# Value products leave PSUM only behind the next pair's global scores, in an order that is searched anew

## The chip, the cores and the metric

One core of one Trainium2 chip runs the kernel. The metric is the device time of one execution in microseconds (us). TensorE (PE) multiplies matrices, VectorE (DVE) and ScalarE (ACT) work elementwise and read PE's results from the eight banks of PSUM, GpSimd (POOL) works elementwise on SBUF only, and SyncE (SP) issues nearly all DMAs from one queue, in order.

## The reference

Eight batches of 8 heads have 512 local and 32 global tokens, head dimension 64. Global tokens attend to all tokens, a local token to the global ones and to its window of 32 to either side. The 4,352 rows of 512 numbers that come out pass an FFN.

```python
s_g = scale * np.matmul(q_g, k_all.transpose(0, 1, 3, 2))
out_g = np.matmul(sm(s_g), v_all)
s_ll = scale * np.matmul(q_l, k_l.transpose(0, 1, 3, 2))
mask = np.abs(pos[:, None] - pos[None, :]) <= window
s_ll = np.where(mask, s_ll, -1000000000.0)
s_lg = scale * np.matmul(q_l, k_g.transpose(0, 1, 3, 2))
a_l = sm(np.concatenate([s_lg, s_ll], axis=-1))
out_l = np.matmul(a_l, np.concatenate([v_g, v_l], axis=2))
...
x = np.ascontiguousarray(attn_out.transpose(0, 2, 1, 3)).reshape(B * S, H * D)
h = x @ w_in
g = h - np.tanh(h)
return (g @ w_out).astype(np.float32)
```

## The kernel before

**Two kinds of work on PE.** The FFN of a batch ("chunk") has steps of 12 matmuls each of 128x512: a step of the hidden layer, H (L1188), and a step of the output layer, O (L1236). Each product is made in three passes from a high and a low half (`x_hi`, `x_lo`, `w_in_hi`, `w_in_lo` and so on). The chunk of batch b runs between the attention steps of batch b+1. Attention goes by pairs of heads. Batches 0 and 1 use the class `Pair`: scores L641, transposes L661, global scores L578, products L738. Batches 2 to 7 use `WindowPair`, and there PE does a **visit** once per pair as one unbroken piece: the value products of the pair in two halves (L1044), then the scores (L874) and the global scores (L896) of the next pair. Between two visits stand 76 to 104 H and O matmuls.

**The banks.** PSUM has two pools: four banks for attention and for H steps, four for the accumulators of O. A visit takes all four of the first: two for the products' halves (named o), two for the scores (s). The global scores of the next pair are written to other columns of the two o banks. A bank goes to an H step when all its readers are done.

**Behind a visit.** `add_output` takes a half of the products out: `high` casts it to `x_hi` (a copy, L368, on ACT or DVE), `rest` subtracts to make `x_lo` (L1077, DVE) and keeps the columns of global tokens in `xg` (L1079, L1081). DVE then finds the peaks of scores (L974) and of global scores (L908), ACT takes exponentials (L982, L938), POOL multiplies by the inverse sums (L996), DVE turns the probabilities (L1014, L963) for the next products. For each H step ACT computes tanh (L1196), DVE subtracts (L1199), ACT or DVE casts `ghi` (L368) and POOL subtracts `glo` (L1205).

**The start.** Weights come in packed pieces: load (L430), rebias on ACT (L437), two shifts on DVE (L441, L445), a cast for the high half (L368) and a subtraction on POOL for the low half (L451). The pieces go through few buffers (`first_q`, `stage`, `wpair`, `wraw`). All of batch 0's attention comes before the first H step.

**What sets the order.** A greedy list scheduler (class `Order`) takes all operations with modelled durations, dependencies (`r`, `w`), banks and buffers, and at each step puts the one that can start first, ties and preferences being set by due times. The due times and penalties come from the table `CFG` of about 190 numbers. In 5 to 72 us of its own clock, where it finds PE without work, it puts dummy matmuls (`fill`, L1843); a fixed number of them stands with the first H step.

**Leaving.** Each chunk's four accumulators are copied out (to halves of `wpair`, two free at a time) and stored by SP (L1264), behind whatever stands in its queue ahead of them: loads of values (L1095 to L1098) and of keys and queries (L843).

## Time and profile before

| | |
|---|---|
| median of 3 runs | 926.34 us (924.04 to 926.7) |
| profiled execution, its own time | 926.6 us |
| span of its profile | 924.8 us |
| PE busy | 908.7 us |
| DVE busy | 703.3 us |
| ACT busy | 409.8 us |
| POOL busy | 331.7 us |
| mean granted clock of TensorE | 0.998 |

The span runs from the first to the last instruction; 1.8 us of the execution lie outside. In the rows below a line of a timeline has start, duration, engine, line, operation, output<-input, and in brackets the idle time before it with what ended it.

### The profile page before, as it was taken

How to read it: one execution, taken by the hardware profiler on the slowest of the kernel's cores; microseconds unless marked ns; L12 is line 12 of the kernel's file. 1: busy time of each engine (PE TensorE's matmuls, PEld its weight loads, DVE VectorE, ACT ScalarE, POOL GpSimd, SP SyncE). 2: the span in 40 equal slices, each digit the busy share in tenths (PEclk: the TensorE clock that was granted, in tenths of full speed). 3: DMA queues.
4: the chain of work that ended last, by engine and by line, in shares of the span. 5: the costliest groups of instructions: out<-in, count | busy, mean ns of one | idle time of the engine just before them, and what ended most of it. 6: DMA issues, size and time to landing. Idle time of an engine off the chain costs nothing.

```text
span 924.8 us, 21774 instructions
## 1 busy us (share of the span) xinstructions
PE 908.7 (98%) x7839; PEld 749.1 (81%) x7839; DVE 703.3 (76%) x2268; ACT 409.8 (44%) x1178; POOL 331.7 (36%) x531
## 2 busy tenths in 40 slices
PE   7989999999999999999999999999999999999998
PEld 5667877788887788878888888888888888898986
DVE  5987776478887877877778787777778787888773
ACT  5976656444344333443334233433334343433232
POOL 3577765733333333332333333333323333110000
PEclk9999999999999999999999999999999999999999
DMA  9556343433234323342324233432324211100001
GB/s 227 143 158 190 117 123 88 95 87 63 59 76 110 64 51 68 63 116 48 62 52 106 51 66 68 98 76 47 71 52 105 48 43 27 46 1 1 1 0 69
DMA packets 248173, 70.13 MB, mean 76 GB/s; under 512 B 232704, under 2 KB 241408, under 8 KB 248064
## 3 DMA queue, kind: packets, MB, share of 16 engines
q1 hardware_dynamic: 246720, 68.21, 31.9%
q8 instruction: 62, 1.02, 0.5%
q10 hardware_dynamic: 1344, 0.52, 0.2%
q14 instruction: 47, 0.39, 0.1%
HBM read 59.77 MB, written 8.91 MB: 74 GB/s over the span
## 4 chain that ended last, share of the span: by engine, by line
PE 91%; DVE 4%; ACT 2%; DMA 1%; SPq 1%; issue 1%; POOL 0%; ACTq 0%; DVEq 0%; POOLq 0%
PE bank L1236 32%; PE bank L1188 31%; PE bank L1561 7%; PE bank L1681 6%; PE bank L1044 5%; PE bank L874 3%; DVE keys_first L1014 2%; PE bank L896 1%; PE bank L641 1%; PE bank L738 1%; PE bank L1587 1%; PE bank L661 1%; PE bank L545 1%; DMA first_raw<-in_q_l_dram 0%; DMA wpair<-in_moe_w_out_dram 0%
## 5 line engine op out<-in xcount | busy, mean ns | idle before, releaser
L1205 POOL TENSOR_TENSOR glo<-t,ghi 128x512 fp32r<-128x512 f32 x112 | 145.6, 1300 | 331.6 <-PE bank L1236 230.1
L1014 DVE STREAM_TRANSPOSE keys_first<-prob 32x256 f32<-32x256 f32 x384 | 167.3, 436 | 9.4 <-POOL prob L996 3.1
L1196 ACT ACTIVATE t<-bank 128x512 f32<-128x512 f32 x112 | 66.9, 597 | 176.9 <-PE bank L1188 162.6
L1236 PE MATMUL bank<-w_out_hi,ghi 128*128 128x512 f32 x448 | 125.0, 392 | 0.7 <-ACT wpair L368 0.7
L1236 PE MATMUL bank<-w_out_hi,glo 128*128 128x512 f32 x448 | 125.0, 393 | 0.1
L1236 PE MATMUL bank<-w_out_lo,ghi 128*128 128x512 f32 x448 | 124.7, 393 | 0.0
L1188 PE MATMUL bank<-x_hi,w_in_hi 128*128 128x512 f32 x448 | 120.6, 391 | 0.9 <-DVE st L974 0.5
L1188 PE MATMUL bank<-x_hi,w_in_lo 128*128 128x512 f32 x448 | 120.2, 390 | 0.0
L1188 PE MATMUL bank<-x_lo,w_in_hi 128*128 128x512 f32 x448 | 120.0, 390 | 0.0
L1199 DVE TENSOR_TENSOR t<-bank,t 128x512 f32<-128x512 f32 x112 | 77.0, 689 | 54.6 <-ACT t L1196 53.1
L368 ACT CAST ghi<-t 128x512 fp32r<-128x512 f32 (+1 forms) x100 | 61.4, 614 | 108.5 <-PE bank L1236 84.1
L1236 PEld LDWEIGHTS bank<-w_out_hi,ghi 128*128 128x128 f32 x448 | 83.3, 188 | 19.9 <-ACT wpair L368 1.4
L1188 PEld LDWEIGHTS bank<-x_hi,w_in_hi 128*128 128x128 f32 x448 | 83.7, 188 | 19.3 <-ACT wpair L437 0.8
L1188 PEld LDWEIGHTS bank<-x_lo,w_in_hi 128*128 128x128 f32 x448 | 84.0, 188 | 18.0 <-issue 0.5
L1236 PEld LDWEIGHTS bank<-w_out_hi,glo 128*128 128x128 f32 x448 | 83.1, 188 | 18.7 <-issue 1.0
L1188 PEld LDWEIGHTS bank<-x_hi,w_in_lo 128*128 128x128 f32 x448 | 83.9, 188 | 17.7 <-issue 0.2
L1236 PEld LDWEIGHTS bank<-w_out_lo,ghi 128*128 128x128 f32 x448 | 83.2, 188 | 18.2 <-issue 0.5
L996 POOL TENSOR_SCALAR prob<-prob,st 128x128 f32<-128x128 f32 x192 | 68.2, 372 | 75.8 <-DVE st L989 48.1
L982 ACT ACTIVATE prob<-prob,st 128x128 f32<-128x128 f32 x192 | 74.7, 391 | 3.6 <-DVE st L974 3.5
L1077 DVE TENSOR_TENSOR x_lo<-bank,x_hi 128x256 fp32r<-128x256 f32 x48 | 20.4, 424 | 49.4 <-ACT x_hi L368 49.4
L1044 PEld LDWEIGHTS bank<-keys_first,values 128*64 128x64 f32 x672 | 42.3, 138 | 9.8 <-DVE t L1199 5.3
L974 DVE CUSTOM_DVE_ANT_0 prob<-bank,wraw 128x128 f32<-128x128 f32 x192 | 45.7, 284 | 4.2 <-PE bank L874 1.6
(250 smaller groups left out, 1512.1 us busy)
## 6 DMA issues: line engine op xcount, KB each, us to landing
out_dram<-wpair SPq DMA_DIRECT2D x28, 256.0 KB, 2.2
rawkq<-in_q_l_dram SPq DMA_DIRECT2D x96, 64.0 KB, 2.3
rawkq<-in_k_l_dram SPq DMA_DIRECT2D x96, 64.0 KB, 2.3
stage<-in_moe_w_out_dram SPq DMA_DIRECT2D x6, 512.0 KB, 4.1
wpair<-in_moe_w_out_dram SPq DMA_DIRECT2D x6, 512.0 KB, 4.1
first_q<-in_moe_w_in_dram SPq DMA_DIRECT2D x6, 512.0 KB, 4.0
stage<-in_moe_w_in_dram SPq DMA_DIRECT2D x6, 512.0 KB, 3.8
values<-in_v_l_dram SPq DMA_DIRECT2D x24, 120.0 KB, 2.3
```

The costliest lines, as they stand in the source:

```text
L368: (nc.scalar.copy if e == "A" else nc.vector.tensor_copy)(dst, src)
L982: nc.scalar.activation(x, x, AF.Exp, bias=s[:, k:k + 1], scale=-1.0, accum_out=s[:, 8 + k:9 + k])
L996: nc.gpsimd.tensor_scalar(x, x, s[:, k:k + 1], 1.0, op0=ALU.mult, op1=ALU.mult)
L1014: nc.vector.transpose(view(win_kf[W * k:W * k + W], [(CH, 2), (P, NT), (1, W)], 3 * G + W * i), src)
L1044: nc.tensor.matmul(dst, win_values[h][:, window(b)], src, start=n == 0, stop=n == len(parts) - 1, skip_group_check=True)
L1188: nc.tensor.matmul(self.h[s][:, j * n:(j + 1) * n], w[:, cc, f * P:(f + 1) * P], self.x()[xi][:, cc, :n], start=part == 0 and cc == 0 and ...
L1196: nc.scalar.activation(tt_[q], self.h[s], AF.Tanh)
L1199: nc.vector.tensor_sub(tt_[q], self.h.pop(s), tt_[q])
L1205: eng[e].tensor_sub(gg[q][1], tt_[q], f32(gg[q][0]))
L1236: nc.tensor.matmul(self.acc[tt], g[:, j * self.n + tt * P:j * self.n + (tt + 1) * P], low_out(f) if wi else high_out(f), start=s == 0 and ...
L1561: nc.tensor.matmul(self.hold(tt, tags), g(), low_out(f) if wi else high_out(f), start=first and k < len(tts), stop=last and k == len(mms) - 1)
L1681: nc.tensor.matmul(dst[:, at], w, m, start=fresh and n == 1, stop=n == 6, skip_group_check=True)
```

## The change

`add_output` gives `high` and `rest` one more operand to wait for: the global scores of the next pair in the same half, where the next pair is of the same batch (`self.jj < 3`). And all numbers of `CFG` are replaced; the core of the diff is below, with one line of the table. One line is added in the code ahead of some places, so that from there on line numbers of the kernel after are one higher (L1189 for L1188, L1237 for L1236).

```diff
-               d_w=0.3761, d_wl=0.2437, d_wn=2.1507, d_xg=1.1595, d_y=3, gfirst=0.0, ho=7017.2009, hs=875.1568, lag=-190.1483,
+               d_w=0.3712, d_wl=0.2437, d_wn=1.8044, d_xg=1.1595, d_y=2.7078, gfirst=0.0, ho=34202.7904, hs=620.2931, lag=-1618.121,
...
             due = self.after(18.0)
-            add(either(256, "ph", True), high, due + 8 * 0.5, r=[o], w=[k + (0,) for k in x])
-            add(("D", 0.6), rest, due + 8 * 1, r=[o] + [k + (0,) for k in x],
+            behind = [("sg", self.j + 1, half)] if self.jj < 3 else []
+            add(either(256, "ph", True), high, due + 8 * 0.5, r=[o] + behind, w=[k + (0,) for k in x])
+            add(("D", 0.6), rest, due + 8 * 1, r=[o] + behind + [k + (0,) for k in x],
```

What the change does to the order is seen in three places.

On DVE, behind a visit of batch 5 whose next pair is of the same batch, before:

```order
L1199 TENSOR_TENSOR t_68<-bank_99,t_68 128x512
L1077 TENSOR_TENSOR x_lo_108<-bank_100,x_hi_107 128x256
L1081 COPY xg<-bank_100 128x32
L1077 TENSOR_TENSOR x_lo_108<-bank_98,x_hi_107 128x256
L1079 TENSOR_TENSOR xg<-bank_98,xg 128x32
L974 ISA prob,st_93<-bank_101,wraw_2008 128x128
L974 ISA st_93 128x1
...
L908 ISA pg,st_93<-bank_100,wraw_2008 128x192
L908 ISA st_93 128x1
L368 CAST ghi_70<-t_68 128x512
```

and after:

```order
L1200 TENSOR_TENSOR t_68<-bank_98,t_68 128x512
L974 ISA prob,st_93<-bank_99,wraw_1989 128x128
L974 ISA st_93 128x1
...
L1077 TENSOR_TENSOR x_lo_108<-bank_101,x_hi_107 128x256
L1081 COPY xg<-bank_101 128x32
L368 CAST ghi_70<-t_68 128x512
L1077 TENSOR_TENSOR x_lo_108<-bank_100,x_hi_107 128x256
L1079 TENSOR_TENSOR xg<-bank_100,xg 128x32
L908 ISA pg,st_93<-bank_101,wraw_1989 128x192
L908 ISA st_93 128x1
```

The subtractions L1077 stood ahead of the four peaks L974 and now stand behind them, ahead of the peaks L908 of the global scores.

On PE, at the first H step (`x_hi_87` is batch 0's activations; L661 and L641 are transposes and scores of a pair of batch 1), before:

```order
L616 MATMUL bank_98<-idr,pg 128x64 x6
...
L1843 MATMUL bank_101<-mask_90 128x224
...
L1188 MATMUL bank_101<-x_hi_87,w_in_hi 128x512 x4
L1188 MATMUL bank_101<-x_lo_88,w_in_hi 128x512 x4
L661 MATMUL bank_100<-idr,prob 128x64
...
L1188 MATMUL bank_101<-x_hi_87,w_in_lo 128x512 x4
L641 MATMUL bank_98<-first_kw_63,first_q_84 128x224
...
L1188 MATMUL bank_99<-x_hi_87,w_in_hi 128x512 x4
```

and after:

```order
L616 MATMUL bank_100<-idr,pg 128x64 x6
L661 MATMUL bank_99<-idr,prob 128x64
...
L641 MATMUL bank_101<-first_kw_63,first_q_84 128x224
...
L1844 MATMUL bank_99<-mask_90 128x224
...
L1189 MATMUL bank_99<-x_hi_87,w_in_hi 128x512 x4
L1189 MATMUL bank_99<-x_lo_88,w_in_hi 128x512 x4
L1189 MATMUL bank_99<-x_hi_87,w_in_lo 128x512 x4
L1189 MATMUL bank_98<-x_hi_87,w_in_hi 128x512 x4
L1189 MATMUL bank_98<-x_lo_88,w_in_hi 128x512 x4
L1189 MATMUL bank_98<-x_hi_87,w_in_lo 128x512 x4
```

A set of transposes and a pair of scores stand ahead of the first H step and no longer inside it; two H steps follow on each other. Over the whole start there are 65 dummy matmuls ahead of the first H step, in ten places, and 81 in eight before.

On PE, between the last O step of batch 0's chunk (`w_out_hi_1492`, after `w_out_hi_1600`, is the last piece of the weights) and the first O step of batch 1's (its four accumulators are the banks 102 to 105), before:

```order
L1236 MATMUL bank_103<-w_out_hi_1492,glo_71 128x512
L1188 MATMUL bank_100<-x_hi_107,w_in_hi 128x512 x4
L1188 MATMUL bank_100<-x_lo_108,w_in_hi 128x512 x4
L1188 MATMUL bank_100<-x_hi_107,w_in_lo 128x512 x4
L1188 MATMUL bank_99<-x_hi_107,w_in_hi 128x512 x4
...
L1188 MATMUL bank_99<-x_hi_107,w_in_lo 128x512 x4
L1236 MATMUL bank_105<-w_out_hi,ghi_72 128x512
L1236 MATMUL bank_104<-w_out_hi,ghi_72 128x512
L1236 MATMUL bank_102<-w_out_hi,ghi_72 128x512
L1236 MATMUL bank_103<-w_out_hi,ghi_72 128x512
```

and after:

```order
L1237 MATMUL bank_105<-w_out_hi_1600,ghi_70 128x512
...
L1237 MATMUL bank_104<-w_out_hi_1600,glo_71 128x512
L874 MATMUL bank_98<-first_m,hi_106 32x128
...
L896 MATMUL bank_100<-first_m,win_gq 32x2x64
...
L1237 MATMUL bank_103<-w_out_hi,ghi_72 128x512
L1237 MATMUL bank_102<-w_out_hi,ghi_72 128x512
L1237 MATMUL bank_105<-w_out_hi,ghi_72 128x512
L1237 MATMUL bank_104<-w_out_hi,ghi_72 128x512
```

Two H steps lay between the two O steps, now a set of scores (L874) and global scores (L896) does. On SP's queue the rows around the stores of batch 0's chunk are the same in both.

## Rows read from the trace of the kernel before

**Rows 1.** The page, part 1: busy time, share, instructions.
```profile
PE 908.7 (98%) x7839; PEld 749.1 (81%) x7839; DVE 703.3 (76%) x2268; ACT 409.8 (44%) x1178; POOL 331.7 (36%) x531
```

**Rows 2.** Stretches: length, busy PE, PEld, DVE, ACT, POOL, PEclk, DMA share, GB/s.
```profile
0.00:50.00 50.00, 40.79 (x404) 29.76 (x405) 37.36 (x165) 38.43 (x127) 26.38 (x59) 1.00 0.72 172
50.00:100.00 50.00, 49.49 (x322) 38.76 (x322) 40.30 (x89) 33.56 (x78) 34.57 (x33) 0.97 0.61 174
```

**Rows 3.** Timeline of TensorE ahead of and at the first FFN step.
```profile
58.38 1.90 PE L1843 MATMUL bank<-mask 128*128 128x224 bf16 x18
60.05 0.94 PE L1188 MATMUL bank<-x_hi,w_in_hi 128*128 128x512 f32 x3
```

**Rows 4.** Waits of TensorE: us in total, times, longest.
```profile
PE bank L545 <- DMA first_raw<-in_k_l_dram: 4.3, 1, 4.3
...
PE bank L1236 <- ACT wpair L368: 0.7, 2, 0.3
PE bank L1044 <- DVE keys_first L1014: 0.6, 1, 0.6
...
PE bank L1188 <- ACT wpair L437: 0.4, 1, 0.4
```

**Rows 5.** Chain in a visit of batch 5, TensorE: start, us, what.
```profile
531.42 1.09 PE bank L874 x64
532.50 0.55 PE bank L896 x25
...
535.09 1.13 PE bank L1188 x5
```

**Rows 6.** Timeline of ScalarE in this visit: start, us, instruction.
```profile
530.60 0.37 ACT L368 CAST x_hi<-bank 128x256 fp32r<-128x256 f32 x1 [2.18 <-PE bank L1044]
```

**Rows 7.** Timeline of VectorE in this visit.
```profile
531.00 0.42 DVE L1077 TENSOR_TENSOR x_lo<-bank,x_hi 128x256 fp32r<-128x256 f32 x1 [1.86 <-ACT x_hi L368]
...
531.90 0.42 DVE L1077 TENSOR_TENSOR x_lo<-bank,x_hi 128x256 fp32r<-128x256 f32 x1 [0.34 <-ACT x_hi L368]
...
532.54 0.29 DVE L974 CUSTOM_DVE_ANT_0 prob<-bank,wraw 128x128 f32<-128x128 f32 x1
...
533.39 0.35 DVE L908 CUSTOM_DVE_ANT_0 pg<-bank,wraw 128x192 f32<-128x192 f32 x1
...
534.90 0.08 DVE L908 DVE_READ_ACCUMULATOR2_ANT st<- 128x1 f32 x1
```

**Rows 8.** Stretches between two visits, columns as in rows 2.
```profile
257.15:278.11 20.96, 20.96 (x229) 17.35 (x228) 18.60 (x69) 9.29 (x30) 7.50 (x13) 1.00 0.46 92
...
427.47:452.06 24.59, 24.59 (x245) 20.35 (x245) 19.80 (x72) 9.42 (x30) 8.08 (x14) 1.00 0.29 57
```

**Rows 9.** Timeline of TensorE: last products, first output step of batch 1.
```profile
172.40 1.10 PE L738 MATMUL bank<-keys_first,values 128*64 128x160 f32 x16
...
188.09 1.07 PE L1188 MATMUL bank<-x_hi,w_in_lo 128*128 128x512 f32 x4
189.00 1.07 PE L1236 MATMUL bank<-w_out_hi,ghi 128*128 128x512 f32 x4
```

**Rows 10.** Chain from 55 to 66 us.
```profile
56.90 0.35 DVE first_q L441
...
57.28 0.70 DVE first_q L445
...
62.78 0.65 PE bank L661 x16
...
64.56 0.96 PE bank L641 x8
```

**Rows 11.** Timeline of SP's queue.
```profile
172.96 0.31 SPq L1095 DMA_DIRECT2D values<-in_v_l_dram  x1
...
184.90 0.91 SPq L1264 DMA_DIRECT2D out_dram<-wpair  x2
```

**Rows 12.** Timeline of ScalarE at the boundary.
```profile
187.33 1.29 ACT L368 COPY wpair<-bank 128x512 f32<-128x512 f32 x2 [0.19 <-DMA out_dram<-wpair]
```

More of the change, by code (lines that the diff above doesn't have):

```diff
@@ new lines @@
+    CFG = dict(win=-2037.3448, a_g=1.5394, a_kg=0.0286, a_ph=0.0761, a_qs=0.5, a_w=0.504, a_wn=0.3721, a_xg=7.3446, d_g=3.5299,
+               d_gl=1.6793, d_kg=1.0548, d_kq=0.1607, d_ph=0.9707, d_pl=3.1864, d_qh=27.4739, d_qs=0.0, d_tg=1.082, d_tp=0.7083,
+               d_w=0.3712, d_wl=0.2437, d_wn=1.8044, d_xg=1.1595, d_y=2.7078, gfirst=0.0, ho=34202.7904, hs=620.2931, lag=-1618.121,
+               last=-56.3309, o_st0=-2882.9568, o_st1=-14793.7625, o_tw0=-13272.045, o_tw1=6650.1542, one=0.0, p0=1139.2524,
+               pen=0.4378, penp=47.4685, s_g=0.7714, s_gl=20.2886, s_kq=73.0039, s_p=1.9417, s_tg=0.5596, s_w=0.0503, s_wl=12.2887,
+               step=1870.9905, step1=472.4061, lag0=-614.8604, hs0=409.7325, tol=0.0788, xs=0.0732, xw=1.719, o_ld0=-570.1206,
+               o_tn0=22442.3855, o_sg0=4325.2829, o_tg0=-34180.6888, o_s0=-23892.643, o_sp0=22263.0481, o_t0=-18361.554,
+               o_tpp0=39998.7697, o_vl0=14689.5993, o_vl1=-13752.6557, o_pv0=26662.3693, o_pvp0=15041.3274, o_ld1=45032.1689,
+               o_pv1=26755.3985, o_pvp1=-14885.4337, o_s1=-4246.7416, o_sg1=-17754.2178, o_sp1=1631.1449, o_t1=-37844.3661,
+               o_tg1=-11506.1568, o_tn1=6097.6172, o_tpp1=-17670.0448, ho0=11666.3692, o_tg=2149.4869, o_pv=1266.5023,
+               o_pvp=-608.8611, o_s=-973.7784, o_sp=-468.8434, o_t=-622.5358, o_tpp=348.926, o_tn=-382.6256, o_ld=423.028,
+               o_lq=846.3999, o_sg=-1214.8469, o_st=-26.0002, o_tw=1592.5009, o_vl=-2037.6091, o_gl=-12.6939, a_kw=0.2609,
+               d_kw=1.0519, s_kw=0.0614, wdi=4791.8912, wdo=3588.6717, L_a_g=0.2008, L_a_kg=6.9738, L_a_ph=0.2364, L_a_qs=197.4661,
+               L_a_w=3.3975, L_a_wn=6.4235, L_a_xg=4.0116, L_d_g=0.3945, L_d_gl=0.5557, L_d_kg=0.1783, L_d_kq=1.1326, L_d_ph=0.531,
+               L_d_pl=8.7171, L_d_qh=0.7611, L_d_qs=907.9411, L_d_tg=8.6488, L_d_tp=8.6984, L_d_w=0.4061, L_d_wl=7.1153,
+               L_d_wn=0.8306, L_d_xg=0.6352, L_d_y=0.2026, L_ho=5490.2678, L_hs=725.9427, L_lag=-3974.7421, L_last=0.1662,
+               L_pen=0.2526, L_penp=1.0537, L_s_g=32.6974, L_s_gl=4.8181, L_s_kq=0.3525, L_s_p=0.5472, L_s_tg=0.3595, L_s_w=1.024,
+               L_s_wl=6.2232, L_o_tg=10203.4279, L_o_pv=1091.7044, L_o_pvp=-908.8877, L_o_s=784.704, L_o_sp=12.1302, L_o_t=-296.8916,
+               L_o_tpp=5.6777, L_o_tn=0.4074, L_o_ld=1344.5838, L_o_lq=1.0773, L_o_sg=-1418.022, L_o_st=0.7565, L_o_tw=1.9187,
+               L_o_vl=2.5326, L_o_gl=2.7771, L_a_kw=0.6919, L_d_kw=0.7466, L_s_kw=0.1786)
```

19 lines of the change are left out of this document (removed).

## Prediction

> **What bounds the kernel now.** I read the busy shares first. TensorE (PE) is busy for 908.7 of 924.8 us [rows 1], so all its idle time together is 16 us, and no order of the same work can save more than that and its dummy matmuls. The stretches say where most of it lies [rows 2]: 9.2 us in the first 50 us, 0.5 in the next 50. Before the first FFN matmul at 60.05 us the scheduler has also put 81 dummy matmuls; the 18 of them right ahead of it take 58.38 to 60.05 us, 0.093 us each [rows 3], so the 81 are worth 7.5 us. After 60 us the waits that matter here are 0.7 us for output copies, 0.6 for the probability turns of L1014 and 0.4 at the first FFN step [rows 4]. So the kernel is bound by PE's work, ahead of 60 us by the chain that makes batch 0's activations, and a change of order pays only at these few places.
>
> Then the visit, the place that the change is named after [rows 5 to 7], here one of batch 5. PE does the value products, the next pair's scores to 532.50, its global scores to 533.05, then O matmuls; the next H step starts at 535.09 [rows 5]. ScalarE (ACT) casts the first product half at 530.60 [rows 6]. VectorE (DVE) waits 1.86 and 0.34 us for these casts, subtracts at 531.00 and 531.90, and starts the peaks at 532.54, just when PE ends the scores [rows 7]. So before the change the evictions sit in DVE time that is idle anyway.
>
> **The change part by part.** Nothing is added to or removed from the arithmetic. I go through the stretches in which the order moves something that PE could wait for.
>
> *The added wait.* ACT's two casts must now follow the global scores: 533.05 in place of 530.60, behind the copy of `first_m`, which ACT does first and which I count like one cast. DVE now does the four peaks first, to about 533.47 (533.39, where L908 took over, + 0.08), then x_lo, xg, a cast of ghi, x_lo, xg, then the L908 peaks. With 0.37 us for the copy and as much for a cast [rows 6] the first cast ends about 533.85, so DVE idles some 0.4 us; then it has two subtractions of 0.42, two xg of half that, a cast of about 0.4 and twice 0.43 of L908 [rows 7], which ends near 536.4, where it ended at 534.98 before (534.90 + 0.08): 1.4 us later. What is queued behind it: on DVE the rest of the softmax and the turns L1014, for which the next visit's products wait; on ACT the exponentials L982; and the two banks of the products, which can go to an H step only when L908 has read them. The banks: the next H step (535.09) takes a scores bank, whose peaks end sooner than before; the one behind it needs a product bank 2.72 us later, near 537.8, so 1.4 us remain. Cost zero, cover 1.4 us. The turns: they end before their visit where PE's work between visits is long. The windows show how full DVE is: between the visits at 257.15 and 278.11 it works 18.60 of 20.96 us, between 427.47 and 452.06 19.80 of 24.59 [rows 8]. In the new order 1.4 us more are needed behind each visit whose next pair is of the same batch, 18 of 24. Against this the searched order spreads FFN matmuls: between the first six visits there stand 92, 92, 80, 88, 96 in place of 84, 84, 76, 88, 88, and later 92 and 100 in turn in place of 88 to 104. Four H or O matmuls are 0.907 us (188.09 to 189.00) [rows 9], so the tight third interval gains 0.9 us and needs 1.4 more, and the others gain or have room. I add +0.5 there and take back 0.3 of the 0.6 us of turns [rows 4], since the first two intervals grow by 1.8 us each and hand over less backlog: +0.2, between -0.6 (the wait goes) and +6 (late turns at most of these visits, below).
>
> TensorE wrote the global scores into a bank whose other columns DVE read from 531.90 to about 532.5 [rows 7], around its start of that work (532.50), and PE's work stays the chain through it, with no wait between scores and global scores [rows 5]. So I put the end of this overlap at nothing; if each overlap had held PE for 0.1 us, 18 of them would give back 1.8. The Trainium skill, "PSUM — Partial Sum Buffer", section "PSUM bank collisions raise a hardware error", says that the hardware neither arbitrates nor stalls when TensorE writes and VectorE reads one bank, but raises an error. By that rule the sum gets 0 here as well, and the point of the wait is another than time. No row here shows that error.
>
> *The start.* Ahead of the first H step stand 65 fillers in place of 81 (16 x 0.093 = 1.5 us less), and one more set of 16 transposes and a pair of scores, 0.65 and 0.96 us of real work that before stood between the first H steps [rows 10]. If the chain to the first activations takes as long, H starts 0.1 us later with 1.6 us more done: -1.5. But one more piece of weights is prepared ahead of batch 0's last activation; on DVE that costs 0.35 + 0.70 us [rows 10]. If all of that is on the chain, -0.5. PE's first FFN step already waits 0.4 us for ACT's work, which shows that the chain counts. I take -1.0, for ends of -5 (the chain loses more than the fillers, see the first rival) and +1.
>
> Clock: in 50 to 100 us the granted clock averages 0.97, and 1.00 in the 50 before [rows 2], so 1.5 us of full speed were lost there in one stretch at 1.2 GHz. The fillers stand in ten places now, in eight before; a second such stretch would cost another 1.5 us, and the sum takes none. The Trainium skill, "TensorE: Matmul & The Clock Gate", Part 1, says that the array falls to half rate when it has been idle and comes back only under work. The trace agrees so far as its one slow stretch lies in the startup, where PE idles.
>
> *The boundary between batch 0's and batch 1's FFN.* Two of the four output copies find a free buffer, the other two must wait until the first two are stored. The stores stand in SP's queue behind the 16 loads of values, of which the first waits for the last products of L738. Before: products at 172.40 [rows 9], first load 172.96, stores issued 184.90 [rows 11], ACT's two held copies at 187.33 to 188.62 [rows 12], the first O step of the new batch at 189.00 [rows 9], so that its third and fourth matmul (0.45 and 0.68 later) just find their banks. Now only scores and global scores lie between the last O step of one and the first of the next. From those products PE needs 1.1 for themselves, 52 x 0.227 = 11.8 for FFN matmuls and 1.09 + 0.55 [rows 5] for both kinds of scores, 14.5 us to the first O step, where it was 16.6. SP's queue has the same rows, so the copies end 15.6 and 16.2 us behind the products; the third matmul is ready at 14.95 and the fourth must still follow: PE waits about 1.1 us. The trace has this event once already, at a later change of chunk: twice 0.3 us of idle PE until output copies, 0.7 in all [rows 4]; there the order is unchanged. +1.1, from 0 (SP's loads start sooner) to +2.
>
> *Everything else*: the later chunk boundaries, the tail and the counts of matmuls, evictions and DMAs are as before: 0.
>
> **Sum**: -1.0 + 0.2 + 1.1 = +0.3 on the profiled 926.6 us, so 926.9. That run is 0.3 above the median of 926.34; on the median it is 926.6, and I say 926.5.
>
> **The rivals.**
> *A, faster: the startup shrinks as a whole.* The only large slack on PE is there: 9.2 us idle, 4.3 of them for the first load, so 4.9 that an order can reach, and 7.5 of fillers. If a third of these 12.4 us goes, and the boundary wait is no longer than 0.5, the time is 926.3 - 4 + 0.5 + 0.2 = 923.0. For it: fewer fillers and more real work ahead of the first H. Against: one more piece of weights on DVE, which carries the chain.
>
> *B, slower: DVE becomes the bound between visits.* Place: the turns L1014 ahead of the products. Each of 18 visits moves 1.4 us of DVE work out of an idle gap into the stretch that must end before the next visit. If the new spacing covers two thirds of them, and 6 wait 0.9 us, that is +5.4, and 926.3 + 5.4 - 1.0 + 1.1 = 931.8; half of it gives 929. It decides when turns end over 0.3 us behind the O matmuls in more than three intervals. For it: the 257 to 278 interval has only 2.4 us of idle DVE [rows 8], and 0.6 us of this wait is already there [rows 4]. Against: in 427 to 452 4.8 us are idle.
>
> *C, slower: weights late.* In the new order the load of the third weight piece of w_in is issued only when GpSimd (POOL) has used the buffer's first piece, and that stands behind batch 0's last probabilities; so PE's third H step comes to depend on it. An H step is 2.7 us (three times 0.907), so a piece late by half a step in three steps gives +4, 930.5. Against it: PE waits for weights nowhere behind its first step now [rows 4].
>
> *D, the change does not act*: casts and subtractions are as before hidden, the boundary wait doesn't come, the start stays: 926.3. It falls into "same" together with the forecast.
>
> **Chances and range.** A measurement of this kernel can tell 0.3%, 2.8 us, from no change. Forecast 0.33, D 0.13, A 0.30, B 0.15, C 0.09. A lies mostly beyond the bound: with a little of the forecast's lower end, faster 0.29. B and C mostly beyond theirs: slower 0.23. Same 0.48. The range takes in A down to 921.5 (a startup shorter by 6) and B and C up to 931.0; the likeliest one's own range is 924.5 to 929.
>
> **What would show it.** In the changed profile: in a visit DVE's peaks at the end of the scores and x_lo about 1.3 us behind the first of them; fewer L1843, first H within 1 us of 60; idle PE near 190 released by output copies (about 0.7 idle, 1.1 in starts); waits for L1014 of no more than 1 us. I am wrong if the first H comes before 57 or after 62, if PE waits for L1014 at several visits, or if the first H steps wait for w_in.

## The result and the profile after

The changed kernel takes 933.12 us (median of 6 runs, 932.89 to 934.55), the kernel before beside it on the same chip 925.84 us (6 runs, 924.04 to 927.58). The ratio is 1.0083, with an interval of 1.0072 to 1.0094: slower by 7.3 us, and above the range of the prediction. The profiled execution of the changed kernel took 934.55 us, with a span of 932.8 us, 8.0 more than before.

The page of the changed kernel says at once that the 8.0 us are not work (part 1, busy time and share):

```profile
PE 910.1 (98%) x7823; PEld 749.5 (80%) x7823; DVE 706.5 (76%) x2258; ACT 413.1 (44%) x1192; POOL 330.4 (35%) x527
```

Its windows say where they lie (columns as in rows 2):

```profile
0.00:50.00 50.00, 39.67 (x376) 28.09 (x378) 34.34 (x156) 35.39 (x117) 23.89 (x56) 0.97 0.67 161
50.00:100.00 50.00, 45.50 (x319) 35.48 (x315) 33.70 (x93) 32.84 (x83) 28.56 (x31) 0.93 0.55 156
36.00:42.00 6.00, 5.20 (x52) 4.03 (x54) 3.09 (x11) 2.89 (x10) 4.53 (x9) 0.72 0.30 99
60.70:64.20 3.50, 3.28 (x24) 2.38 (x25) 1.26 (x5) 1.74 (x6) 3.50 (x5) 0.56 0.93 239
64.20:67.30 3.10, 2.45 (x15) 2.03 (x15) 2.77 (x12) 2.96 (x11) 0.25 (x1) 0.50 0.84 260
```

PE's busy time grew by 1.4 us only, against [rows 1]. In 50 to 100 us PE worked 45.50 us where it worked 49.49 [rows 2], and the granted clock fell from 0.97 to 0.93. The short windows show where: from 60.70 to 67.30 us the clock was granted at 0.56 and 0.50, so for nearly all of that time PE ran at 1.2 GHz, and for part of 36 to 42 us too.

The waits of PE in the changed kernel (in total, times, longest), to be held against [rows 4]:

```profile
PE bank L738 <- DMA values<-in_v_g_dram: 2.6, 1, 2.6
PE bank L661 <- POOL prob L719: 2.6, 2, 2.5
...
PE bank L896 <- issue: 1.1, 2, 0.8
PE bank L1189 <- ACT w_in_hi L368: 1.0, 1, 1.0
PE bank L1844 <- ACT keys_first L368: 0.7, 1, 0.7
...
PE bank L1237 <- ACT wpair L368: 0.4, 2, 0.2
```

The wait of L1044 for the turns (the transposed probabilities) has left this list, though not the kernel (see "The turns" below), and the one for output copies (wpair) is 0.4 us in place of 0.7. Others have come, and the largest stand in the start. The timeline of PE there (start, duration, in brackets the idle time before and its releaser):

```profile
36.80 1.98 PE L738 MATMUL bank<-keys_first,values 128*64 128x160 f32 x16 [2.65 <-DMA values<-in_v_g_dram]
...
57.64 0.58 PE L616 MATMUL bank<-idr,pg 64*128 64x64 f32 x6
60.71 0.28 PE L661 MATMUL bank<-idr,prob 64*128 64x64 f32 x2 [2.49 <-POOL prob L719]
61.14 1.44 PE L661 MATMUL bank<-idr,prob 64*128 64x64 f32 x14 [0.15 <-POOL prob L719]
62.37 1.85 PE L641 MATMUL bank<-first_kw,first_q 64*128 64x224 f32 x8
64.87 2.77 PE L1844 MATMUL bank<-mask 128*128 128x224 bf16 x14 [0.65 <-ACT keys_first L368]
67.32 1.46 PE L1189 MATMUL bank<-x_hi,w_in_hi 128*128 128x512 f32 x4
...
70.46 0.84 PE L1189 MATMUL bank<-x_hi,w_in_hi 128*128 128x512 f32 x3
```

The first H step starts at 67.32 us and not at 60.05 [rows 3]. Read from 57.64 on, PE is idle for 2.49 us, until GpSimd has the probabilities for the transposes L661 that the new order put there. Then everything takes twice its time: 14 transposes 1.44 us and the scores L641 1.85, where 16 transposes and the scores took 0.72 and 1.03 us on the timeline of the kernel before; the 14 dummy matmuls, behind another 0.65 us of waiting for ScalarE, 0.198 us each (2.77 by 14) against 0.106 (1.90 by 18) [rows 3].

The first pass of H needs x_lo of batch 0 only in its second part. On VectorE, and at the other ends of the two waits (GpSimd and ScalarE), one reads:

```profile
61.45 0.42 DVE L749 TENSOR_TENSOR x_lo<-bank,x_hi 128x256 fp32r<-128x256 f32 x1
...
60.20 1.73 POOL L719 TENSOR_SCALAR prob<-prob,st 128x224 f32<-128x224 f32 x4 [2.18 <-DVE st L713]
...
63.68 0.67 ACT L437 ACTIVATE wpair<-wpair 128x512 f32<-128x512 f32 x1 [1.38 <-DMA wpair<-in_moe_w_out_dram]
64.25 1.05 ACT L368 COPY keys_first<-bank 128x512 f32<-128x512 f32 x2
```

And in the chain the load that ScalarE waits for:

```profile
58.05 5.61 DMA wpair<-in_moe_w_out_dram
```

Batch 0's last x_lo starts at 61.45 us, and in the kernel before at 61.28: the activations are as early as they were, and H comes 7.27 us later because it stands behind the transposes and scores in PE's order. The 0.65 us come about so: ScalarE stands until 63.68 us at a rebias of a piece of w_out, whose load was issued at 58.05 and took 5.61 us to land (last row); the two copies behind it are what the dummy matmuls wait for.

From there I followed the lag, the time of a visit after minus the time of the same visit before, less 0.2267 us for each H or O matmul that the one has done more. It is 9.4 us at the first visit (216.42 against 211.59, with 504 such matmuls in place of 524), falls to 6.9 at the fifteenth, jumps there by 1.1 and four visits later by 0.6, and is 8.0 at the end. The jumps are the `L896 <- issue` gaps above, 0.75 and 0.31 us of idle PE in the middle of the global scores and what follows on them. The fall has two parts. 1.4 us of it come in one step, from the fifth visit to the sixth: at the fifth, at 302.96, the value products of the kernel before waited for turns and took 3.09 us in place of 1.88, and here they do not. The rest is 0.2 us behind most visits whose next pair is of the same batch. The chain through one visit shows what it is (start, duration, what):

```profile
536.67 1.88 PE bank L1044 x56
538.56 1.09 PE bank L874 x64
539.64 0.36 PE bank L896 x28
540.00 2.02 PE bank L1237 x8
```

The global scores cost the chain 0.36 us here; before they cost 0.55 [rows 5]. At this place the added wait saves PE 0.19 us in each of 18 visits, 3.4 us in all; what it costs elsewhere in the visit stands under "The turns".

### The profile page after: what moved, and what is told of

Read it like the earlier page. It is cut to its first block, busy times and chain, and to the rows that moved or that the text cites. A ratio compares the mean times of both kernels' runs of the same rounds, so it can differ in the third digit from the quotient of the medians.

```text
span 932.8 us, 21738 instructions
## 1 busy us (share of the span) xinstructions
PE 910.1 (98%) x7823; PEld 749.5 (80%) x7823; DVE 706.5 (76%) x2258; ACT 413.1 (44%) x1192; POOL 330.4 (35%) x527
## 3 DMA queue, kind: packets, MB, share of 16 engines
q8 instruction: 62, 1.02, 0.5%
## 4 chain that ended last, share of the span: by engine, by line
PE 89%; DVE 4%; DMA 3%; ACT 1%; issue 1%; POOL 1%; SPq 1%; ACTq 0%; DVEq 0%; POOLq 0%
PE bank L1189 31%; PE bank L1237 31%; PE bank L1562 7%; PE bank L1682 6%; PE bank L1044 5%; PE bank L874 3%; DVE keys_first L1014 1%; PE bank L738 1%; PE bank L896 1%; PE bank L641 1%; PE bank L1588 1%; DMA wpair<-in_moe_w_out_dram 1%; PE bank L545 1%; PE bank L661 1%; DMA first_q<-in_moe_w_in_dram 1%
## 5 line engine op out<-in xcount | busy, mean ns | idle before, releaser
L1014 DVE STREAM_TRANSPOSE keys_first<-prob 32x256 f32<-32x256 f32 x384 | 167.1, 435 | 7.6 <-POOL prob L996 1.1
L1197 ACT ACTIVATE t<-bank 128x512 f32<-128x512 f32 x112 | 67.0, 598 | 179.7 <-PE bank L1189 176.1
L1237 PE MATMUL bank<-w_out_hi,ghi 128*128 128x512 f32 x448 | 125.6, 394 | 0.9 <-DVE w_out_hi L368 0.4
L1237 PE MATMUL bank<-w_out_lo,ghi 128*128 128x512 f32 x448 | 125.0, 393 | 0.3 <-POOL w_out_lo L451 0.3
L1237 PE MATMUL bank<-w_out_hi,glo 128*128 128x512 f32 x448 | 123.8, 391 | 0.0
L1189 PE MATMUL bank<-x_hi,w_in_hi 128*128 128x512 f32 x448 | 121.2, 392 | 1.5 <-ACT w_in_hi L368 1.0
L1189 PE MATMUL bank<-x_lo,w_in_hi 128*128 128x512 f32 x448 | 120.1, 390 | 0.0
L1189 PE MATMUL bank<-x_hi,w_in_lo 128*128 128x512 f32 x448 | 120.1, 390 | 0.0
L368 ACT CAST ghi<-t 128x512 fp32r<-128x512 f32 (+1 forms) x113 | 69.5, 615 | 104.5 <-PE bank L1237 51.4
L1189 PEld LDWEIGHTS bank<-x_hi,w_in_hi 128*128 128x128 f32 x448 | 83.7, 188 | 20.7 <-ACT w_in_hi L368 1.4
L1237 PEld LDWEIGHTS bank<-w_out_hi,ghi 128*128 128x128 f32 x448 | 83.0, 188 | 19.9 <-ACT wpair L368 1.2
L1189 PEld LDWEIGHTS bank<-x_lo,w_in_hi 128*128 128x128 f32 x448 | 83.9, 188 | 18.0 <-issue 0.5
L1237 PEld LDWEIGHTS bank<-w_out_hi,glo 128*128 128x128 f32 x448 | 83.7, 188 | 18.2 <-issue 0.6
L1189 PEld LDWEIGHTS bank<-x_hi,w_in_lo 128*128 128x128 f32 x448 | 83.9, 188 | 17.8 <-issue 0.3
L1237 PEld LDWEIGHTS bank<-w_out_lo,ghi 128*128 128x128 f32 x448 | 83.1, 188 | 18.4 <-POOL w_out_lo L451 0.6
L974 DVE CUSTOM_DVE_ANT_0 prob<-bank,wraw 128x128 f32<-128x128 f32 x192 | 45.6, 283 | 52.4 <-PE bank L874 51.9
L1044 PEld LDWEIGHTS bank<-keys_first,values 128*64 128x64 f32 x672 | 42.7, 138 | 9.5 <-DVE keys_first L1014 3.6
L1044 PE MATMUL bank<-keys_first,values 128*64 128x32 f32 (+2 forms) x672 | 48.1, 228 | 0.2
```

Of the source, the lines that this page charges most:

```text
L368: (nc.scalar.copy if e == "A" else nc.vector.tensor_copy)(dst, src)
L1014: nc.vector.transpose(view(win_kf[W * k:W * k + W], [(CH, 2), (P, NT), (1, W)], 3 * G + W * i), src)
L1044: nc.tensor.matmul(dst, win_values[h][:, window(b)], src, start=n == 0, stop=n == len(parts) - 1, skip_group_check=True)
L1189: nc.tensor.matmul(self.h[s][:, j * n:(j + 1) * n], w[:, cc, f * P:(f + 1) * P], self.x()[xi][:, cc, :n], start=part == 0 and cc == 0 and ...
L1197: nc.scalar.activation(tt_[q], self.h[s], AF.Tanh)
L1237: nc.tensor.matmul(self.acc[tt], g[:, j * self.n + tt * P:j * self.n + (tt + 1) * P], low_out(f) if wi else high_out(f), start=s == 0 and ...
```

## The experiments

Two theories stand against each other. By the first (S in the expectations) the loss is made in the start, by the order that the new table gives, and the added wait is a gain. By the second (V) the wait costs, by late turns or otherwise, and the table is harmless. Rivals within the first: the values loaded late, the rebias in ScalarE's way, or the place of the extra transposes and scores.

To hold an order fixed, a list of what the scheduler had picked (operation, engine, earliest start) is played back ahead of its own search. In the cuts below the list itself is replaced by a few words in brackets:

```diff
+        first = list(FIRST)
         while left:
             best = None
-            for o in ready if forced is None else [forced]:
+            want = first.pop(0) if first else None
+            for o in [self.ops[want[0]]] if want else ready if forced is None else [forced]:
...
+                    if want and e != want[1]:
+                        continue
```

**Which half of the change.** Four kernels, run together beside the kernel before (925.87).

The changed kernel with the order of before up to the first visit, and the new table behind it:

```diff
+FIRST = (picks of the kernel before, up to its first visit)
```

> The order of before up to the first visit, behind it the wait and the new table. Theory S (the time was lost ahead of the first visit, in the order of the start; behind it the wait pays about 0.2 us per visit, since the global scores no longer wait for VectorE's subtraction): the first visit at 211.6 us as before, and the end 1 to 4 us ahead of before, 922 to 925 us. Theory V (the wait makes the visits late, and the start's loss would have been given back): 930 us or more, with turns late at the visits.

Measured: 930.91 us, 1.0053 (1.004 to 1.0065). The lag is 0.0 at the first visit, so the start's loss is gone, and falls by 0.2 a visit up to the third. But the scheduler, whose earlier intervals had become longer, left only 60 H and O matmuls ahead of the fourth visit, and PE waits 4.4 us for turns there; that, the half clock behind it and small gaps bring the lag to 4.4 at the end.

The kernel before with the wait alone:

```diff
+            behind = [("sg", self.j + 1, half)] if self.jj < 3 else []
-            add(either(256, "ph", True), high, due + 8 * 0.5, r=[o], w=[k + (0,) for k in x])
-            add(("D", 0.6), rest, due + 8 * 1, r=[o] + [k + (0,) for k in x],
+            add(either(256, "ph", True), high, due + 8 * 0.5, r=[o] + behind, w=[k + (0,) for k in x])
+            add(("D", 0.6), rest, due + 8 * 1, r=[o] + behind + [k + (0,) for k in x],
```

> The table of before with the wait added, nothing else; the scheduler orders anew behind the first visit. Theory S: global scores take 0.40 us in place of 0.59 in 18 visits, 3.5 us less, minus up to 2.5 us where turns come late, since this table leaves no more room for them: 922 to 925 us. Theory V: 1.4 us more work of VectorE behind each visit makes turns late at six or more of them, 928 to 932 us.

Measured: 933.09 us, 1.0084 (1.007 to 1.0097). The same place decides, again with 60 matmuls in the interval ahead of the fourth visit. Among the waits of PE:

```profile
PE bank L1044 <- DVE keys_first L1014: 6.1, 6, 4.4
```

And two windows (columns as in rows 2), ahead of that visit and in it:

```profile
276.15:280.57 4.42, 0.00 (x1) 0.00 (x1) 4.26 (x11) 1.17 (x2) 0.00 (x0) 1.00 0.65 230
280.57:284.40 3.83, 3.82 (x56) 3.34 (x56) 1.40 (x4) 0.37 (x1) 0.00 (x0) 0.55 0.08 26
```

PE idles 4.42 us and then gets its clock at 0.55 for the whole of the value products. The lag goes from -1.9 to 3.8 over this visit and the next. Behind that the value products take 2.0 to 2.7 us at eleven visits in place of 1.88, some 5 us in all, which is more than the wait gives back; the lag is 5.0 at the end. So the wait without a fitting table costs as much as the whole change, by late turns, most of it at the one interval that the search made short. The time lies above the ranges of both theories.

The new table with no wait:

```diff
-            behind = [("sg", self.j + 1, half)] if self.jj < 3 else []
+            behind = []
```

> The new table without the wait. Theory S: the start of after, first FFN matmul near 67 us, and visits with global scores of 0.59 us: 2 to 4 us slower than after, 935 to 937 us. Theory V: faster than after, 926 to 929 us.

Measured: 933.77 us, 1.0092 (1.0077 to 1.0106). The lag is 9.9 at the first visit, 9.3 at the sixth and still 9.3, without a change, at the twenty-third: the 0.2 a visit belong to the wait, and nearly all of the loss is there at the first visit. The global scores are as before:

```profile
541.83 0.55 PE bank L896 x25
```

By medians the wait in the new table is worth 0.65 us only (933.77 to 933.12, not run side by side; the intervals of the two ratios overlap). In the profiles two things that this kernel doesn't have take back its 3.4: the issue gaps 1.7, and late turns inside the value products 1.8 (below).

The kernel before with the new start:

```diff
+FIRST = (picks of the changed kernel, up to its first visit)
```

> The order of after up to the first visit, behind it the old table and no wait. Theory S: the first visit 5 us later than before at 20 FFN matmuls less, that is 9 us late, and nothing of it is given back: 934 to 936 us. Theory V: the loss of the start is mostly given back, 926 to 929 us.

Measured: 938.84 us, 1.0152 (1.0133 to 1.0171): a lag of 7.2 at the first visit, 9.9 at the fourth and 12.1 at the fifth, by late turns and half clock behind them, and 11.6 to 11.7 from the sixth on. The new start alone costs 7 us.

**The wait with nothing else moved, and the parts of the start.** Four kernels beside the kernel before (924.78).

The order of before throughout; on ScalarE and VectorE alone the evictions of 18 visits stand behind the global scores and the first peaks, as in the changed kernel. One such visit on VectorE:

```diff
-L1077 TENSOR_TENSOR x_lo<-bank,x_hi 128x256
-L1081 COPY xg<-bank 128x32
-L1077 TENSOR_TENSOR x_lo<-bank,x_hi 128x256
-L1079 TENSOR_TENSOR xg<-bank,xg 128x32
 L974 ISA prob,st<-bank,wraw 128x128
...
+L1077 TENSOR_TENSOR x_lo<-bank,x_hi 128x256
+L1081 COPY xg<-bank 128x32
+L1077 TENSOR_TENSOR x_lo<-bank,x_hi 128x256
+L1079 TENSOR_TENSOR xg<-bank,xg 128x32
 L908 ISA pg,st<-bank,wraw 128x192
```

> The order of before on TensorE, GpSimd and SyncE, row for row; on ScalarE and VectorE only the evictions of the 18 visits are moved behind the global scores and the first peaks. Theory R (two terms: global scores 0.19 us shorter in each of 18 visits, 3.5 us in all; and 1.4 us more work between a visit and its turns, which costs where the turns of before had less room than that, the visits near 234, 257, 278, 328, 378 and 757, some 0.3 + 1.1 + 1.4 + 0.2 + 0.8 + 0.2 = 4.0 us): no change, 925 to 928 us, with the waits for turns at those visits and nowhere else. Rival (VectorE becomes the bound at most visits): over 930 us.

Measured: 921.17 us, 0.9959 (0.9947 to 0.9972), the fastest of all kernels here. Line numbers are 6 higher in it (L902 for L896, L1050 for L1044). The chain in a visit and the one wait for turns:

```profile
528.70 0.36 PE bank L902 x28
```

```profile
PE bank L1050 <- DVE keys_first L1020: 0.2, 1, 0.2
```

The global scores cost 0.36 us, and with 84, 84, 76 and 88 matmuls in the first intervals the turns are waited for 0.2 us, less than before. The lag falls from -1.1 to -5.5: by 0.2 at most visits, and by 0.5 and 0.9 at two places where the kernel before waits for turns and for output copies. The -1.1 at the first visit is the start of this one profile, which has no stretch at half clock (1.00 in 50 to 56 us, against 0.72 before). Of the executions with a mean clock of 1.00 alone this kernel took 920.84 to 921.38 us and the one before 923.99 to 924.49, so the gain is not the clock's. It was not expected: the theory put the late turns at 4.0 us, and they did not come.

The changed order, with the load of a w_out piece behind four loads of queries and values in SP's queue, its rebias behind the exponentials on ScalarE, and 5 more dummy matmuls:

```diff
-L430 DMA stage<-in_moe_w_out_dram 128x1024
 L529 DMA rawkq<-in_q_l_dram 128x4x64 x2
...
 L1151 DMA values<-in_v_g_dram 32x6x64
+L430 DMA stage<-in_moe_w_out_dram 128x1024
```

> The order of after, in which one load of weights on SyncE (at 27.85 us) goes behind the four loads of queries and values that follow it, and its rebias on ScalarE behind the next three sets of exponentials. Theory Q (the start is lost in queues: TensorE's 2.6 us for values at 36.8 are one of its places): TensorE does its products near 34.3 in place of 36.8, and the first FFN matmul comes 1 to 2.4 us sooner, 930.5 to 932.5 us in the end. Rival (the chain of VectorE sets the first FFN step, the values have room): first FFN matmul at 67 us and 933 us as after.

Measured: 929.63 us, 1.005 (1.0033 to 1.0067), 3.5 less than the changed kernel (3.1 by the two ratios; the changed kernel was not run beside these four). PE still waits 1.4 us for values, but reaches L616 at 53.18 us in place of 57.64. From there to the first H it needs 9.1 us, where the changed kernel needs 9.7: the repair acts ahead of that place.

The changed order, with the rebias of `wpair` behind the two copies that wait behind it:

```diff
-L437 ACTIVATE wpair<-wpair 128x512
 L368 COPY keys_first<-bank 128x2x4x64
 L368 COPY keys_first<-bank 128x2x4x64
+L437 ACTIVATE wpair<-wpair 128x512
```

> The order of after, in which ScalarE's rebias of one piece of weights (at 63.7 us, it waits for its load) stands behind the two copies of transposed probabilities that free a bank for the first FFN step. Nothing else moves. Theory Q: the copies come at 62.3 in place of 64.3, the fillers and the first FFN matmul 1 to 2 us sooner, 931 to 932.5 us. Rival: first FFN matmul unchanged, 933 us.

Measured: 932.87 us, 1.0085 (1.0069 to 1.01): no gain. H starts 8.2 us behind L616 in place of 9.7, so the move acts, but it is partly taken back 16 us later (L1197 is H here):

```profile
62.67 1.33 PE L1197 MATMUL bank<-x_hi,w_in_hi 128*128 128x512 f32 x4
...
78.99 1.20 PE L1197 MATMUL bank<-x_hi,w_in_hi 128*128 128x512 f32 x4 [1.79 <-ACT w_in_hi L376]
```

The fourth H step, which starts at 78.99, waits 1.79 us for a piece of w_in, where the changed kernel waits 1.00 ahead of 82.97, and behind it two passes of four matmuls run at half clock (1.84 and 1.91 us in place of 1.07). This is the place of rival C: the weights cap what an earlier first step can win. (L616 itself is 3.2 us earlier in this profile, at 54.46, in the same order; this spread of the start is in the profiles and not in the medians; more on it under "What stays open".)

The changed order, with the first H step ahead of the extra transposes and scores, 9 more dummy matmuls:

```diff
 L616 MATMUL bank<-idr,pg 128x64 x6
-L661 MATMUL bank<-idr,prob 128x64
...
-L641 MATMUL bank<-first_kw,first_q 128x224
...
 L1844 MATMUL bank<-mask 128x224
 L1189 MATMUL bank<-x_hi,w_in_hi 128x512 x4
 L1189 MATMUL bank<-x_lo,w_in_hi 128x512 x4
 L1189 MATMUL bank<-x_hi,w_in_lo 128x512 x4
+L661 MATMUL bank<-idr,prob 128x64
...
+L641 MATMUL bank<-first_kw,first_q 128x224
```

> The order of after, in which the first FFN step stands ahead of the extra set of transposes and scores, as it does before the change. Theory Q (batch 0's activations are ready near 62 us as they are in before; TensorE comes to them late only because it stands, in order, at transposes that wait for GpSimd and at fillers that wait for ScalarE): first FFN matmul at 61 to 63 us in place of 67.3, and 3 to 4 us less in the end, 929 to 930.5 us. Rival (what follows, the third weight piece, takes it back): the first FFN matmul sooner, but the wait for the high half of w_in near 82 grows and 932 to 933.5 us.

Measured: 927.62 us, 1.0028 (1.0015 to 1.0041), 5.5 less than the changed kernel (5.1 by the two ratios). Its timeline of PE (L1195 is H, L667 the transposes, L647 the scores):

```profile
57.13 0.95 PE L1195 MATMUL bank<-x_hi,w_in_hi 128*128 128x512 f32 x3
...
58.96 1.09 PE L1195 MATMUL bank<-x_lo,w_in_hi 128*128 128x512 f32 x4
...
60.88 0.72 PE L667 MATMUL bank<-idr,prob 64*128 64x64 f32 x16
...
61.92 1.37 PE L647 MATMUL bank<-first_kw,first_q 64*128 64x224 f32 x8
```

The 16 transposes take 0.72 us and wait for nothing, and the clock is granted at 1.00 from 50 to 100 us. In this profile L616 already starts at 54.75, 2.9 us ahead of the changed kernel's, in an order that is the same up to there; that much of its lead in the profile is the start's spread and not the repair's.

**Three tests of what that left.** Beside the kernel before (925.18).

The order of before, with only the second half's evictions behind the global scores, the first half's where they were. The reason for this kernel is in the program: of the 32 global scores of a visit every second one writes to the bank of the second half, which VectorE must have read. In the trace of the kernel before 48 weight loads of L896 carry a wait for VectorE, two per visit, in the changed one 11.

```diff
 L1081 COPY xg<-bank 128x32
-L1077 TENSOR_TENSOR x_lo<-bank,x_hi 128x256
-L1079 TENSOR_TENSOR xg<-bank,xg 128x32
 L974 ISA prob,st<-bank,wraw 128x128
...
+L1077 TENSOR_TENSOR x_lo<-bank,x_hi 128x256
+L1079 TENSOR_TENSOR xg<-bank,xg 128x32
 L908 ISA pg,st<-bank,wraw 128x192
```

> As the kernel that only moves evictions in the order of before, but only the second half's cast, subtraction and copy of global columns go behind the global scores; the first half's stay where they were. Theory W (TensorE's second global score waits for VectorE to have read the second half's bank, since the instruction carries a wait for VectorE; the first half's bank has been read long before): the whole gain stays, 921 to 922.5 us, global scores 0.40 us. Rival (reading PSUM beside TensorE slows it, whichever half): half of the gain at most, 923 us or more.

Measured: 922.51 us (12 runs), 0.9971 (0.9962 to 0.998). L904 is L896 here, in the chain and among the waits:

```profile
531.03 0.36 PE bank L904 x28
```

```profile
PE bank L904 <- DVE xg L1089: 0.5, 2, 0.3
```

The global scores cost 0.36 us with half the evictions moved, so what held PE was the second half's alone. Two visits, with 0.3 us at most, still wait for VectorE's `xg` of the first half. The gain is 2.7 us, against 3.6 with both halves moved; the two intervals overlap.

The changed kernel with both repairs of the start, the values first and the first H step first:

```diff
-FIRST = (picks of the changed kernel)
+FIRST = (the same, with both moves shown above)
```

> The order of after with two repairs of its start together: the values load ahead of a load of weights on SyncE, and the first FFN step ahead of the extra transposes and scores. Theory Q (both are places of one loss, and behind the start the new order is ahead of before by 1 to 2 us): the two gains, 3.5 and 5.5 us, add up in part, 923 to 926 us. Rival (both end at the same later wait, a weight piece): no better than the second repair alone, 927.5 us.

Measured: 925.78 us (11 runs), 1.0005 (0.9995 to 1.0014): the time of the kernel before, 7.3 less than the changed one. Lag 1.6 at the first visit, 0.1 at the end. The two repairs won 3.5 and 5.5 alone, and 7.3 together (3.1, 5.1 and 7.2 by the ratios).

The mirror of the last repair: the order of before, with one set of transposes and scores put ahead of the first H step, as the change has it, and 13 more dummy matmuls:

```diff
-L1188 MATMUL bank<-x_hi,w_in_hi 128x512 x4
-L1188 MATMUL bank<-x_lo,w_in_hi 128x512 x4
 L661 MATMUL bank<-idr,prob 128x64
...
-L1188 MATMUL bank<-x_hi,w_in_lo 128x512 x4
 L641 MATMUL bank<-first_kw,first_q 128x224
...
+L1188 MATMUL bank<-x_hi,w_in_hi 128x512 x4
+L1188 MATMUL bank<-x_lo,w_in_hi 128x512 x4
+L1188 MATMUL bank<-x_hi,w_in_lo 128x512 x4
```

> The order of before, in which the set of transposes and scores that stands inside the first FFN step goes ahead of it, as the change has it. Nothing else is moved; the scheduler adds some 13 fillers around it. Theory Q: TensorE waits at the transposes for GpSimd to 62.6 us, the first FFN matmul comes 3 to 5 us later with 1.6 us more done, 927 to 930 us. Rival (the set's place costs nothing): 925 to 926.5 us.

Measured: 929.8 us, 1.0056 (1.004 to 1.0071), 4.6 more than before, by this move and the dummy matmuls that come with it. Of the 31 behind L616 16 run while GpSimd's probabilities are not there yet, and 14 stand ahead of H, where 18 stood. Its timeline (L669 transposes, L1851 dummy matmuls, L1196 H):

```profile
56.26 0.59 PE L624 MATMUL bank<-idr,pg 64*128 64x64 f32 x6
...
59.92 0.28 PE L669 MATMUL bank<-idr,prob 64*128 64x64 f32 x2 [1.44 <-POOL prob L727]
...
64.41 2.80 PE L1851 MATMUL bank<-mask 128*128 128x224 bf16 x14
66.88 1.58 PE L1196 MATMUL bank<-x_hi,w_in_hi 128*128 128x512 f32 x4
```

The changed kernel's picture comes back: a wait for GpSimd, then dummy matmuls at 0.2 us each, H at 66.88. The lag is 5.3 at the first visit and 4.8 at the end.

One number sums the start up, the time from L616 to the first H step. It is 2.2 to 2.5 us in all seven kernels that put H first (the one before among them, 57.86 to 60.05), and 8.2 to 10.6 in all six that put the set first. The times themselves were foreseen less well than the places: six of the eleven lie outside every range that was written down.

## Why the prediction was wrong

**The start** is the step that failed: "If the chain to the first activations takes as long, H starts 0.1 us later with 1.6 us more done", the term -1.0 with bounds of -5 and +1. Its condition held, since x_lo came at 61.45 and 61.28, and its conclusion did not. I priced the moved transposes and scores by their durations, 0.65 and 0.96 us, and not by when their inputs are ready. PE works in order, so H waits behind them: 2.49 us for GpSimd, 0.65 for ScalarE, 0.15 in between. From L616 to H that makes 9.68 us in place of 2.19. The 7.5 us between are 1.6 of moved work, 3.3 of waits and 2.7 of half clock (next point), less 0.4 for 4 dummy matmuls fewer, which gives 7.2. The lag was 7 us at 83 us, behind the wait for w_in, 8 at 188.91, and with the waits of the boundary (below) 9.4 at the first visit; so the term that was put at -1.0 measured about +8. That this placing is the cause is shown both ways: taken out it gives back 5.5 us, put into the kernel before it costs 4.6. The values waited for at 36.80 us are the second part: without most of that wait the kernel gains 3.5 us. The prediction did not see it at all, and the time of L616 hides it, which is no later than before (57.64 and 57.86) with 16 dummy matmuls fewer.

**The clock.** "A second such stretch would cost another 1.5 us, and the sum takes none": it came, twice. By the windows 60.70 to 67.30 alone lost 3.28 x 0.44 + 2.45 x 0.50 = 2.7 us of full speed, and the other stretch, 0.72 in 36 to 42 us, follows the 2.65 us of idle PE ahead of 36.80. The Trainium skill, "TensorE: Matmul & The Clock Gate", Part 1, has the array at half rate after idling; the rows of this kernel agree, for behind both of these waits the granted clock is between 0.50 and 0.72. But not every wait of the start was followed by such a stretch: behind 1.93 us of idle PE at the same values the kernel with the first H step first kept 1.00 up to 50 us, and so did the one with the old table and the new start behind 2.04. The kernel before fell to 0.72 in 50 to 56 us behind idle stretches of 1.26 and 0.88 us, and the one with moved evictions kept 1.00 behind 1.17 and 0.91 at the same place. I used the page to explain the one stretch that was there, and not to ask behind which new wait there would be a next one.

**The added wait** was put at +0.2 with nothing for the end of the overlap, because "PE's work stays the chain through it, with no wait between scores and global scores". The chain, the busy time and PE's list of waits do not show this wait, since it sits inside a run of pipelined matmuls, near the first of 32. The 0.55 us of [rows 5] were 0.36 of work and 0.19 of waiting for VectorE's `xg` of the second half: in the trace of before that copy ends at 532.44, and of the 32 global scores the first starts at 532.25 and the third at 532.50. It is the same at all 23 visits that have both products and global scores: the weight load that is held starts 0.05 us behind the end of that copy, and in the changed kernel only at the five visits whose next pair is of another batch. The real term of this place is -3.4; the text's own bound, 1.8, was too short by half. The Trainium skill, "PSUM — Partial Sum Buffer", section "PSUM bank collisions raise a hardware error", says that the hardware does not stall on such an overlap; the runs do not contradict it, since the program itself carries the wait. The constant 0.05 us leaves little room for a contention in that bank beside it.

**The turns.** VectorE was to end 1.4 us later in a visit. It ended 0.5 later, by the last L908 at 6.0 us behind the visit's start where it was at 5.5: I had added whole durations (0.42 for x_lo), while the next instruction starts 0.34 behind it. VectorE in the changed visit:

```profile
539.68 0.29 DVE L974 CUSTOM_DVE_ANT_0 prob<-bank,wraw 128x128 f32<-128x128 f32 x1 [3.40 <-PE bank L874]
...
540.70 0.42 DVE L1077 TENSOR_TENSOR x_lo<-bank,x_hi 128x256 fp32r<-128x256 f32 x1
541.04 0.20 DVE L1081 COPY xg<-bank 128x32 f32<-128x32 f32 x1
...
542.55 0.08 DVE L908 DVE_READ_ACCUMULATOR2_ANT st<- 128x1 f32 x1
```

The peaks start with the end of the scores and x_lo 1.02 us behind the first of them, where 1.3 was said. PE's list of waits names no turn in the changed kernel. But the value products hold such waits inside, as the global scores did (a visit's products take 1.88 us elsewhere, see the chain above):

```profile
664.06 2.12 PE bank L1044 x49
```

There the last turn ends at 664.39 us and the weight load that is held starts at 664.44. It is 0.24 us at five visits, 0.43 at 385.46 and 0.60 at 287.18, 2.2 us in all; the kernel before has 1.8 at two visits, of which the prediction, by [rows 4], counted 0.6, and the table alone has 0.4 at one. The waits of the weight loads, which run ahead of the matmuls, have the same order (changed kernel, before, table alone):

```profile
PEld bank L1044 <- DVE keys_first L1014: 3.6, 11, 0.4
PEld bank L1044 <- DVE keys_first L1014: 2.6, 7, 0.8
PEld bank L1044 <- DVE keys_first L1014: 0.6, 2, 0.4
```

So in the new table the wait made turns late by 1.8 us, half of what it won, and rival B came, in small. Its mechanism grows where an interval is short: 60 matmuls made an idle stretch of 4.4 us (the wait alone, and the old start with the new table), 76 one of 0.2.

**The boundary** of batch 0 and 1 was to cost 1.1 us (0.7 of idle). No output copy is waited for there at all (the 0.4 us stand at 406 us, at a later change of chunk, as before), and other waits stand there that I had not foreseen:

```profile
188.91 0.47 PE L1237 MATMUL bank<-w_out_hi,ghi 128*128 128x512 f32 x1 [0.44 <-DVE w_out_hi L368]
189.64 0.50 PE L1237 MATMUL bank<-w_out_lo,ghi 128*128 128x512 f32 x1 [0.25 <-POOL w_out_lo L451]
...
195.70 1.13 PE L874 MATMUL bank<-first_m,hi 64*32 64x128 f32 x63 [0.57 <-DVE first_m L848]
```

0.69 us for the last pieces of w_out, 0.57 for `first_m`. PE is that much later there; that the copies are in time for this reason is argued and was not tried.

**The rivals.** A named the right place with the wrong sign. B came at a third of its price and beside a larger loss (above). C named the right weights (the fourth H step waits for them, not the third), and they act as a cap: 1.0 us in the changed kernel, 1.8 where the first H came sooner. All three signs that would show the prediction wrong came: the first H behind 62 us, an H step that waits for w_in, and, inside the products, waits for L1014 at several visits.

**What stays open.** The issue gaps in the global scores: they stand in six kernels, all of them with the new table and the added wait together, up to 1.5 us in one; neither the table alone nor the moved evictions alone have them, and no row here names their cause. And the spread of the start: L616 began at 57.64, 54.75 and 54.46 us in three kernels with the same order up to there. Part of it is seen: the first of them, the changed kernel, lost 1.7 us at half clock in 36 to 42 us, where the two others were granted 1.00, and waited 2.65 us for values, where they waited 1.93 and 1.71.

## What to carry to other kernels

When an order is changed, ask of each instruction that moves up on an in-order engine when its last input is ready, not how long it takes: here 1.6 us of real work moved ahead cost some 5. A wait in the startup can be paid twice on TensorE, once as idle time and once at half clock behind it: here 3.3 us of waits and 2.7 of half clock. And a good local move should be tried with the old order played back around it before the whole order is searched anew: the moved evictions in the old order made the kernel faster (921.17 us), and the new search hid that under a loss.

## What the runs showed of the hardware

A run of small matmuls can hold a wait that TensorE's own list of waits does not count: 32 global scores took 0.55 us of the chain with a wait near the first, and 0.36 without, and the value products of a visit 2.12 and 1.88, while PE counted as busy in all of them. Comparing the same group in two kernels shows it, and for the products so does the list of waits of the weight loads (PEld). Behind idle stretches of 2.49, 2.65 and 4.42 us TensorE was granted between 0.50 and 0.72 of its clock over the next 4 to 7 us, dummy matmuls included; behind 1.93 and 2.04 us in two other kernels it stayed at 1.00. And the landing time of a 512 KB weight piece was 4.3 us (before, issued at 35.36) and 5.6 us (after, at 58.05), and the second time ScalarE waited 1.38 us of that.
